# Another search for the order of 18,000 instructions in a one-core attention and MLP kernel

## The chip, the cores and the metric

The kernel runs on one core of a Trainium2 chip. A core has five engines with a queue of instructions each: TensorE (PE in the rows; its weight loads are PEld), VectorE (DVE), ScalarE (ACT), GpSimd (POOL) and SyncE (SP, which here only issues DMAs). The metric is the device time of one execution in microseconds (us), smaller is better. The kernel before takes 666.7 us (median of 3 runs, 666.36 to 667.87).

## The reference

Three layers over a sequence of S = 576 rows, 4 batches, 8 heads of 64 features (512 in all):

```python
def attn(q, k, v):                       # B, H, S, D = 4, 8, 576, 64; scale = 1/8
    q_d, k_d, v_d = (mean over groups of 4 rows)           # 144 rows
    out_up = repeat(softmax(scale * q_d @ k_d.T) @ v_d, 4)
    scores = where(abs(i - j) < 4, scale * q @ k.T, -1e9)
    return out_up + softmax(scores) @ v

def moe(x, w_ch1, w_ch2):                # 512 -> 2048 -> 512
    u = x + real(fft(fft(x, axis=1), axis=2))
    un = (u - mean(u)) / sqrt(var(u) + 1e-6)
    return u + maximum(un @ w_ch1, 0) @ w_ch2

def moe2(x, w_val, conv_w, w_out):       # causal convolution of 5 taps over the rows
    gate = sigmoid(conv(x, conv_w))
    return (gate * (x @ w_val)) @ w_out
```

## The kernel before, in words

Features lie on partitions, rows along the free axis. The MLP and what follows work in twelve units of 192 rows, three for each batch. The first unit's MLP (lines 1160 and 1171) takes float32 operands; the other eleven split every operand into two float16 halves and sum three products (lines 1196 and 1216, products of 192 columns).

The weights come as 64-bit floats. A float32 weight is put together out of the two 32-bit words by three VectorE instructions on 128x1024 integers, here called words: a first step, a TENSOR_SCALAR (`word_op`, line 547), and two SCALAR_TENSOR_TENSOR (helper `stt`, line 448). The tiles are W and X (X_125, X_126 and W_118 to W_123 hold raw weights, W_114 to W_117 the first matrix's float32 words).

Before the first unit can start, batch 0 has to pass attention, transform and mean. This start-up is the function `chain0`, and its steps are:

- local attention in three groups of windows, of 64-row products: scores (line 1439, dS, loads of k in kTa and q in X), maximum (1452), exponentials on ScalarE (1462, dP and its sums dsu), norm on VectorE (1467, 1468 and the helper at 451), turn by TensorE (1476, dPT) and copy (1479), values (1495, dO), and the addition to x on VectorE (454);
- coarse attention for four pairs of heads: sums over four rows (1510, qkT), scores (1518, sc), maximum (1525, nm), exponentials on ScalarE (1534, E, sums lsu), norm, turn (1549, eT), copy by ScalarE (1552, ET), values (1558);
- sums over v and a covariance (1572 to 1585, cv) that scale the float16 halves, folds (1601, fF), halves (FH, FL), the transform over features (1627, ab), mirrored rows (1637 and 1638, mir), the transform over rows (1665), the mean (1707, st), and u (1711).

The coarse norm is the one step of this part that runs on GpSimd (G); V is VectorE:

```python
def coarse_norm(a):
    s_, E = lr["su", a], lr["E", a]
    V.tensor_scalar(out=s_, in0=s_, scalar1=1e-9, scalar2=None, op0=ALU.add)
    V.reciprocal(out=s_, in_=s_)
    for par in range(2):
        mul(G, E[:, par], E[:, par], s_[:, par].unsqueeze(2).to_broadcast([QC, 2, SD]))
```

The order in which every engine works is not left to a scheduler. The program is built as a list of 692 parts, each a step of this kind, and a table ORDER holds for each of the five engines a list of part numbers (`n.a-b` takes the instructions a to b of part n on that engine). Each instruction is chained behind the one ahead of it in that list by a dependency that needs no semaphore. So the table is the order of the five queues, and the waits between engines come on top from the data.

```python
    for name, eng in engines.items():
        line = []
        for x in ORDER[name].split():
            ...
        for x, y in zip(line, line[1:]):
            tc.add_manual_dep(y, x.name, mybir.DependencyInfo(
                mybir.DependencyClass.NoSync, mybir.DependencyReason.DATA), reason="order")
```

Of the kernel before, what the change touches and what calls it, by code (L numbers as in the profile page):

```python
# [80 lines left out]
263.1 296.2 291.2 302 296.1 291.3 394.0 265.0 288.3 265.2 298.3 265.1 288.0 263.3 265.3 306 315 267.0-1 319 269.0-1  # L81
295.0 267.2 269.2 296.0 301 327 272.0 288.1 272.1 274.0 288.4 274.1 288.5 298.2 275.0 288.2 275.1 311 298.0-1 289.3
277.0-1 289.0 277.2 289.1 289.4-5 289.2 277.3 278 394.1 283.0-1 318.0-1 283.2 334 330 283.3-4 286.0 291.4 286.1-2
342.0 314 342.1 318.2 283.5 303.0 305.0 283.6 290.2 290.1 320.1 346 320.3 290.0 318.3 321.1 321.3 303.1 320.0 320.2
323.1 305.1 349 321.0 331 325.0 324 356 321.2 323.3 323.0 323.2 325.1 326.3 326.1-2 326.0 333 394.2 363 339.0 336.0
339.1-2 336.1 325.2-3 347.0 347.3 347.2 337.1 337.0 339.3 348.3 348.2 348.0 351.0 370 394.3 351.2 347.1 339.4 348.1
339.5-7 358 351.3 337.2-3 378 384 353.2-3 339.8-9 368.3 394.4 351.1 368.0 353.0-1 339.10 388 316 368.1 368.4 368.2
368.5 369.0 372.3 396 372.0 364.0 369.1 374.0 393.0 364.1 372.1-2 372.4-5 393.1 400.1 402.1 376.0 374.1 376.3 383.2-3
405 399 376.1 406.1 376.2 376.4-5 380.3 380.0 400.0 400.3 416 413 380.1 402.0 380.2 380.4-5 374.2-3 426 374.4 383.0
406.0 390.0 383.1 387.0-1 418 391.0 429 387.2 390.1 391.2 390.2 391.1 390.3 387.3 391.3 390.4 395.1 395.0 390.5-6  # L90
398.0-1 395.2 390.7 398.2 390.8 522.0 432 390.9 400.2 404 446.1 374.5 435 402.3 402.2 410.1 406.2-3 374.6 390.10 408
439 407 446.0 410.0 410.3 441 410.2 411.0 411.2 411.1 443 522.1 411.3 430.0 414 457 423.0 436.0-1 423.1 428.1 428.0
430.1 449 446.2 436.2-3 422 436.4 428.2 455 428.3 436.5 434.1 444.1 436.6 434.0 444.3 436.7 425 447.1 458 444.0 444.2
462 436.8 447.0 447.3 447.2 450.3 450.2 450.1 522.2 453.3 450.0 453.2 453.1 436.9-11 434.2-3 453.0 451.1 451.0 463.0
460.0 436.12-13 466 468 460.1 522.4 436.14 451.2-3 473 463.1 478 483.0 486.3 486.0 489 480 481.0 486.4 486.1 486.5
481.3 481.2 488.3 427 492.3 492.0 486.2 483.1-2 504 483.3 492.1 499 483.4 488.2 492.4 492.2 492.5 495.0 503 483.5-8
488.0 490.3 497.3 497.0 495.1 509 506.2 483.9 522.3 497.4-5 497.1-2 495.2 490.0 490.2 481.1 502.3 502.0 495.3 488.1
483.10 490.1 514 494.3 494.0 506.3 506.0 502.4 495.4 494.1-2 502.1 502.5 502.2 517 506.1 524 521.0 513.0-2 521.1 507.0
# [1832 lines left out]
```

## Time and profile before

| | |
|---|---|
| median of 3 runs | 666.7 us (666.36 to 667.87) |
| the profiled execution | 668.18 us |
| its span in the profile | 666.4 us |
| mean granted TensorE clock | 0.985 of full speed |
| TensorE busy | 647.4 us (97%), 7751 products |
| VectorE, ScalarE, GpSimd busy | 458.3, 328.5, 127.1 us |
| DMA | 52.08 MB, 79 GB/s over the span |

The span is what the profiler saw between the first and the last instruction; the execution's time has 1.8 us more around it. Every position below is in us from the start of the span. Records of one line that follow each other are put into one row of a timeline with their count, and the brackets at its end say how long the engine had been idle and who released it.

### The profile page before, as it was taken

What the parts mean: (1) busy time and instruction counts of PE and PEld (TensorE: products, weight loads), DVE (VectorE), ACT (ScalarE), POOL (GpSimd) and SP (SyncE); (2) the same over time, 40 slices, a digit from 0 to 9 for tenths busy, and PEclk for the clock granted to TensorE, in tenths of its full rate; (3) what the DMA queues carried; (4) which work ended last, traced back from release to release, by engine and by line L of the source; (5) the groups of instructions that cost most, each with busy time, mean ns of one, the idle gap of its engine ahead of it and who ended that gap; (6) DMA issues with size and microseconds to landing.
All of it is one profiled execution on the core that took longest, in us unless ns stands there. A gap on an engine that the chain in (4) does not pass through costs nothing.

```text
span 666.4 us, 18165 instructions
## 1 busy us (share of the span) xinstructions
PE 647.4 (97%) x7751; PEld 581.6 (87%) x7751; DVE 458.3 (69%) x950; ACT 328.5 (49%) x997; POOL 127.1 (19%) x178
## 2 busy tenths in 40 slices
PE   8968999999999999999999999999999999999997
PEld 4647799999998887989988898998999989999895
DVE  3679999989998877657876645675447763562344
ACT  3665577888334757675235576643232313312122
POOL 0240306321210613501110352030001020000000
PEclk9959999999999999999999999999999999999999
DMA  8976072313424001403240020000300000000001
GB/s 301 402 247 243 2 253 82 101 34 100 161 60 171 20 18 46 142 1 104 77 150 2 27 62 17 3 1 25 116 2 17 2 1 33 1 2 18 2 32 48
DMA packets 23299, 52.08 MB, mean 78 GB/s; under 512 B 1855, under 2 KB 11071, under 8 KB 22194
## 3 DMA queue, kind: packets, MB, share of 16 engines
q1 hardware_dynamic: 23218, 50.91, 22.4%
q8 instruction: 61, 1.00, 0.6%
q14 instruction: 20, 0.16, 0.1%
HBM read 44.41 MB, written 8.26 MB: 79 GB/s over the span
## 4 chain that ended last, share of the span: by engine, by line
PE 78%; DVE 11%; issue 5%; DMA 3%; POOL 2%; ACT 1%; SPq 0%; POOLq 0%; ACTq 0%
PE ph L1196 25%; PE pc L1216 24%; PE out L1324 7%; PE val L1308 7%; DVE W L448 5%; PE ab L996 2%; POOL E L451 1%; PE dO L805 1%; PE po L1572 1%; PE st L1080 1%; PE sc L883 1%; DMA raw<-in_moe_w_ch_dram 1%; PE pc L1171 1%; DMA kTa<-in_k_dram 1%; PE dPT L788 1%
## 5 line engine op out<-in xcount | busy, mean ns | idle before, releaser
L1196 PE MATMUL ph<-uh,W 128*128 128x192 f16 x1408 | 198.3, 246 | 1.3 <-DVE hl L448 0.7
L1196 PEld LDWEIGHTS <-W 128*128 128x128 f16 x2112 | 176.8, 98 | 9.5 <-issue 4.3
L1216 PE MATMUL pc<-hh,W 128*128 128x192 f16 x1232 | 171.7, 246 | 0.0
L1196 PE MATMUL ph<-ul,W 128*128 128x192 f16 x704 | 171.2, 246 | 0.0
L1216 PEld LDWEIGHTS <-W 128*128 128x128 f16 x1848 | 154.3, 98 | 5.7 <-issue 1.4
L1216 PE MATMUL pc<-hl,W 128*128 128x192 f16 x616 | 129.5, 246 | 0.0
L1200 ACT ACTIVATE hh<-ph 128x384 f16<-128x384 f32 x88 | 42.7, 488 | 125.8 <-PE ph L1196 100.5
L448 DVE SCALAR_TENSOR_TENSOR hl<-ph,hh 128x384 f16<-128x384 f32 x88 | 48.2, 552 | 77.6 <-ACT hh L1200 77.4
L448 DVE SCALAR_TENSOR_TENSOR W<-X,cw,W 128x192 f32<-128x192 f32 x160 | 64.1, 437 | 2.7 <-ACT W L1271 2.3
L1308 PE MATMUL val<-yy,W 128*128 128x192 f16 x576 | 59.6, 246 | 0.5 <-ACT yy L1250 0.5
L1308 PEld LDWEIGHTS <-W 128*128 128x128 f16 x576 | 48.5, 98 | 1.1 <-issue 0.4
L1324 PE MATMUL out<-W,gh 128*128 128x512 f16 x144 | 46.5, 379 | 0.0
L769 ACT ACTIVATE dP<-dS,dmx 128x64 f32<-128x64 f32 x120 | 36.2, 329 | 0.6 <-PE dPT L788 0.3
L448 DVE SCALAR_TENSOR_TENSOR W<-W,W 128x1024 int32<-128x1024 int32 x24 | 29.5, 1237 | 0.1
L451 POOL TENSOR_TENSOR E<-E,lsu 72x288 f32<-72x288 f32 x16 | 18.9, 1197 | 55.1 <-ACT nm L1529 19.7
L454 POOL TENSOR_TENSOR sq<-sq 128x384 f32<-128x384 f32 (+1 forms) x12 | 10.6, 880 | 93.6 <-ACT sq L1091 93.2
L1324 PE MATMUL out<-W,gl 128*128 128x512 f16 x72 | 27.1, 379 | 0.0
L769 ACT ACTIVATION_READ_ACCUMULATOR dP<-dS,dmx 128x1 f32 x120 | 26.7, 223 | 0.0
L1324 PEld LDWEIGHTS <-gh 128*128 128x128 f16 x144 | 14.0, 98 | 12.0 <-issue 0.2
L1216 PE MATMUL pc<-hh,Wz 128*128 128x192 f16 x176 | 24.3, 246 | 0.0
L1171 PE MATMUL pc<-h,W 128*128 128x192 f32 x128 | 23.3, 329 | 0.0
L1160 PE MATMUL ph<-u,W 128*128 128x192 f32 x128 | 22.5, 327 | 0.4 <-DVE u L1711 0.4
(288 smaller groups left out, 1212.0 us busy)
## 6 DMA issues: line engine op xcount, KB each, us to landing
W<-in_moe_w_ch_dram SPq DMA_DIRECT2D x12, 1024.0 KB
out_dram<-osb SPq DMA_DIRECT2D x17, 256.0 KB
vw<-in_vw_dram SPq DMA_DIRECT2D x8, 512.0 KB
v<-in_vp_dram SPq DMA_DIRECT2D x24, 144.0 KB
X<-in_q_dram SPq DMA_DIRECT2D x6, 576.0 KB
kT<-in_k_dram SPq DMA_DIRECT2D x4, 582.0 KB
X<-in_moe_w_ch_dram SPq DMA_DIRECT2D x2, 1024.0 KB
raw<-in_moe_w_ch_dram SPq DMA_DIRECT2D x4, 512.0 KB
```

Of the source, the lines that this page charges most:

```text
L448: return eng.scalar_tensor_tensor(out=out, in0=in0, scalar=scalar, in1=in1, op0=op0, op1=op1)
L451: return eng.tensor_tensor(out=out, in0=a, in1=b, op=ALU.mult)
L454: return eng.tensor_tensor(out=out, in0=a, in1=b, op=ALU.add)
L769: A.activation(out=s_[:, z, a], in_=pss[par][:, z, a], func=AF.Exp, scale=SCALE, bias=mx[:, par, z, a:a + 1], accum_out=su[:, par, z, a:a ...
L996: T.matmul(out=ps[0:n, c0:c1], lhsT=d[x][:, c, sd, e, n0:n0 + n], rhs=feat[:, w, c, c0:c1], start=(t == 0), stop=(t == 5),)
L1160: T.matmul(out=ps[:, e], lhsT=W[AT[kc * 2 + m // 8] + 1][:, o:o + 128], rhs=u()[:, kc, :], start=(kc == 0), stop=(kc == 3))
L1171: T.matmul(out=c["ps"][m // 2][:, m % 2], lhsT=W[9 + g][:, o:o + 128], rhs=hs[g // 2][:, g % 2, e, :], start=(kk == 0 and m % 2 == 0), sto ...
L1196: T.matmul(out=ps[:, e], lhsT=w1_ap(pw, kc, 2 * g + e), rhs=uh[px][:, kc, :], start=(t == 0), stop=(t == 11))
L1200: A.activation(out=h_, in_=ps, func=AF.Relu)
L1216: T.matmul(out=ps[m // 2][:, m % 2], lhsT=w2_ap(pw, kk, m), rhs=x[px][:, e, :], start=(kk == 0 and (pw, px) == (0, 0) and m % 2 == 0), sto ...
L1308: T.matmul(out=ps[:, e], lhsT=wv_ap(pw, kc, 2 * mh + e), rhs=m_["y"][px][:, kc, :], start=(t == 0), stop=(t == 11))
L1324: T.matmul(out=ps, lhsT=(gh, gl)[px][:, kc, t * 128:(t + 1) * 128], rhs=wo_ap(pw, kc), start=(n == 0), stop=(n == 11))
```

## The change

Only the table ORDER changes: all five lists are other orders of the same parts. No instruction's shape, engine or operands change, and no tile is placed elsewhere. Because the table became 14 lines longer, each line number after it is larger by 14 in the changed kernel. One line of the diff stands for the rest:

```diff
     "vector": """
-21 20 30 18 25 32.0-1 32.3 32.2 41 48.0 38.1 38.0 48.1 28 23 27 58.0 54 65 58.1 0 31 71 77.1 77.0 60 34 81.0 85.0 81.1
...
```

On SP, the second load of k is now asked for ahead of the first of q, the table for the transform over features goes from behind six weight loads to ahead of all of them, and the weight loads change places. GpSimd's coarse norms stay in their order. On TensorE the turns and values of the second and third local groups follow each other as before, and the first mirrored products come ahead of the transform over features, the others in the middle of it.

The first place is VectorE's queue around the last of the four coarse norms (its sums are lsu_552, its reciprocal releases GpSimd), up to the norm of the second local group (dsu_342). W and X are words; f2_v0, f2s_v0, p2a and p2b are one-element-wide steps that find a scale, tot is in PSUM. Before:

```order
L515 TENSOR_REDUCE f2_v0_559<-tot_557 128x1
L1539 TENSOR_SCALAR lsu_552<-lsu_552 72x4
L517 TENSOR_SCALAR f2s_v0_561<-f2_v0_559 128x1
L1540 RECIPROCAL lsu_552<-lsu_552 72x4
L547 TENSOR_SCALAR W1_114<-X_126 128x1024
L547 TENSOR_SCALAR W3_115<-W19_123 128x1024
L448 SCALAR_TENSOR_TENSOR W1_114<-X_126,W1_114 128x1024
L448 SCALAR_TENSOR_TENSOR W3_115<-W19_123,W3_115 128x1024
L547 TENSOR_SCALAR W5_116<-W11_119 128x1024
L448 SCALAR_TENSOR_TENSOR W1_114<-X_126,W1_114 128x1024
L448 SCALAR_TENSOR_TENSOR W5_116<-W11_119,W5_116 128x1024
L1467 TENSOR_SCALAR dsu_342<-dsu_342 128x16
```

And now:

```order
L1553 TENSOR_SCALAR lsu_552<-lsu_552 72x4
L462 SCALAR_TENSOR_TENSOR cw_108<-craw_109,cw_108 128x20
L1554 RECIPROCAL lsu_552<-lsu_552 72x4
L561 TENSOR_SCALAR W5_116<-W9_118 128x1024
L529 TENSOR_REDUCE f2_v0_559<-tot_557 128x1
L531 TENSOR_SCALAR f2s_v0_561<-f2_v0_559 128x1
L462 SCALAR_TENSOR_TENSOR W3_115<-W19_123,W3_115 128x1024
L513 TENSOR_SCALAR p2a_565<-f2s_v0_561 128x1
L462 SCALAR_TENSOR_TENSOR W5_116<-W9_118,W5_116 128x1024
L561 TENSOR_SCALAR W7_117<-W15_121 128x1024
L515 TENSOR_SCALAR p2b_567<-p2a_565 128x1
L1481 TENSOR_SCALAR dsu_342<-dsu_342 128x16
```

Seven word operations stood between the reciprocal and the local group's norm, without anything between them; now there are four, and the scale's small steps stand between them.

The second place is VectorE's queue a little earlier, around the covariance's first reader (tr from cv) and the norms of the second and third coarse pairs (lsu_379, lsu_499). Before:

```order
L547 TENSOR_SCALAR W1_114<-X_125 128x1024
L451 TENSOR_TENSOR tr_459<-cv_414,eye_102 128x128
L1539 TENSOR_SCALAR lsu_379<-lsu_379 72x4
L1540 RECIPROCAL lsu_379<-lsu_379 72x4
L1525 TENSOR_REDUCE nm_478<-sc_472 72x2
L1525 TENSOR_REDUCE nm_478<-sc_473 72x2
L606 TENSOR_REDUCE ss_v0_461<-tr_459 128x1
L470 MEMSET ones_105 128x128
L448 SCALAR_TENSOR_TENSOR W1_114<-X_125,W1_114 128x1024
L1539 TENSOR_SCALAR lsu_499<-lsu_499 72x4
L1540 RECIPROCAL lsu_499<-lsu_499 72x4
```

And now:

```order
L561 TENSOR_SCALAR W1_114<-X_125 128x1024
L462 SCALAR_TENSOR_TENSOR W1_114<-X_125,W1_114 128x1024
L462 SCALAR_TENSOR_TENSOR W3_115<-W17_122,W3_115 128x1024
L1553 TENSOR_SCALAR lsu_379<-lsu_379 72x4
L462 SCALAR_TENSOR_TENSOR cw_108<-craw_109,cw_108 128x20
L561 TENSOR_SCALAR W7_117<-W13_120 128x1024
L465 TENSOR_TENSOR tr_459<-cv_414,eye_102 128x128
L1554 RECIPROCAL lsu_379<-lsu_379 72x4
L484 MEMSET ones_105 128x128
L1539 TENSOR_REDUCE nm_478<-sc_472 72x2
L1539 TENSOR_REDUCE nm_478<-sc_473 72x2
L561 TENSOR_SCALAR W1_114<-X_126 128x1024
```

Words have come ahead of tr. From the start up to the last pair's lsu_552 there are ten word operations (five first steps, five others) where there were four (two and two); reductions still follow the reciprocals of the second and third pair.

The third place is ScalarE's queue around the copies of the last pair's turned E (ET_606, ET_613) and the exponentials of the second local group (dP_344, dP_353). Before:

```order
L1462 ACTIVATE dP_344,dsu_342<-dS_246,dmx_291 128x64 x4
L1462 ACTIVATE dP_353,dsu_342<-dS_248,dmx_291 128x64
L1560 ACTIVATE base_136<-po_594 128x144
L1462 ACTIVATE dP_405,dsu_394<-dS_308,dmx_384 128x64
L1552 ACTIVATE ET_606<-eT_601 72x288
L1462 ACTIVATE dP_353,dsu_342<-dS_248,dmx_291 128x64
L1552 ACTIVATE ET_613<-eT_608 72x288
L1462 ACTIVATE dP_344,dsu_342<-dS_246,dmx_291 128x64 x3
L1462 ACTIVATE dP_353,dsu_342<-dS_248,dmx_291 128x64 x3
L1560 ACTIVATE base_136<-po_615 128x144
```

And now:

```order
L1476 ACTIVATE dP_344,dsu_342<-dS_246,dmx_291 128x64
L1476 ACTIVATE dP_353,dsu_342<-dS_248,dmx_291 128x64 x2
L1574 ACTIVATE base_136<-po_594 128x144
L1566 ACTIVATE ET_606<-eT_601 72x288
L1476 ACTIVATE dP_344,dsu_342<-dS_246,dmx_291 128x64 x2
L1566 ACTIVATE ET_613<-eT_608 72x288
L1476 ACTIVATE dP_344,dsu_342<-dS_246,dmx_291 128x64 x2
L1476 ACTIVATE dP_396,dsu_394<-dS_306,dmx_384 128x64
```

Of the second group's sixteen exponentials four now stand behind the first copy, where seven stood.

## Rows read from the trace of the kernel before

**Rows 1.** The page: busy time of each engine, and TensorE in the 40 slices.
```profile
PE 647.4 (97%) x7751; PEld 581.6 (87%) x7751; DVE 458.3 (69%) x950; ACT 328.5 (49%) x997; POOL 127.1 (19%) x178
...
PE   8968999999999999999999999999999999999997
```

**Rows 2.** The chain that ended last: start us, us, what.
```profile
93.18 7.09 DMA raw<-in_moe_w_ch_dram
...
639.37 5.94 PE pc L1216 x72
```

**Rows 3.** TensorE's waits from 79 us on: us in total, times, longest.
```profile
PE ph L1196 <- DVE hl L448: 0.7, 1, 0.7
...
PE dPT L788 <- DVE dP L451: 0.3, 1, 0.3
```

**Rows 4.** Windows: stretch, us, busy by engine, granted clock, DMA share, GB/s.
```profile
32.00:52.00 20.00, 14.17 (x150) 10.78 (x150) 15.38 (x33) 12.58 (x67) 9.18 (x3) 0.50 0.70 230
54.00:60.00 6.00, 4.16 (x39) 3.11 (x36) 5.92 (x14) 3.04 (x7) 0.00 (x0) 1.00 0.76 271
60.00:70.00 10.00, 9.68 (x115) 8.29 (x113) 10.00 (x15) 6.71 (x15) 0.03 (x1) 1.00 0.66 242
70.00:79.00 9.00, 8.43 (x86) 6.16 (x84) 8.19 (x19) 4.74 (x12) 5.09 (x13) 1.00 0.01 3
130.00:662.00 532.00, 529.91 (x6526) 485.07 (x6525) 351.02 (x776) 246.42 (x707) 91.54 (x134) 1.00 0.14 46
...
45.00:75.00 30.00, 27.14 (x340) 22.16 (x337) 29.70 (x57) 20.28 (x52) 3.08 (x8) 0.88 0.40 145
79.00:127.00 48.00, 47.85 (x458) 46.24 (x458) 46.15 (x59) 33.56 (x101) 14.38 (x16) 1.00 0.38 134
```

**Rows 5.** GpSimd's timeline, 26 to 43 us.
```profile
27.37 1.29 POOL L451 TENSOR_TENSOR E<-E,lsu 72x288 f32<-72x288 f32 x2 [4.96 <-ACT ET L1552]
30.94 2.94 POOL L451 TENSOR_TENSOR E<-E,lsu 72x288 f32<-72x288 f32 x2 [2.28 <-DVE lsu L1540]
34.42 7.30 POOL L451 TENSOR_TENSOR E<-E,lsu 72x288 f32<-72x288 f32 x2 [0.54 <-DVE lsu L1540]
```

**Rows 6.** VectorE's timeline, 26 to 78 us.
```profile
26.65 0.29 DVE L451 TENSOR_TENSOR tr<-cv,eye 128x128 f32<-128x128 f32 x1 [2.58 <-PE cv L1585]
...
27.67 0.82 DVE L1525 TENSOR_REDUCE nm<-sc 72x2 f32<-72x288 f32 x2 [0.44 <-PE sc L1518]
...
33.79 0.16 DVE L515 TENSOR_REDUCE f_v<-tot 128x1 f32<-128x1 f32 x1 [0.44 <-PE tot L509]
...
34.07 0.17 DVE L1540 RECIPROCAL lsu<-lsu 72x4 f32<-72x4 f32 x1
34.17 0.66 DVE L547 TENSOR_SCALAR W<-X 128x1024 int32<-128x1024 int32 x1
...
39.36 1.21 DVE L448 SCALAR_TENSOR_TENSOR W<-W,W 128x1024 int32<-128x1024 int32 x1
44.76 0.18 DVE L1467 TENSOR_SCALAR dsu<-dsu 128x16 f32<-128x16 f32 x1 [4.19 <-ACT dP L1462]
...
77.99 0.95 DVE L1711 TENSOR_TENSOR u<-X,st 128x768 f32<-128x768 f32 x1 [0.40 <-PE st L1707]
```

**Rows 7.** TensorE's timeline, 41 to 80 us.
```profile
41.15 1.32 PE L1549 MATMUL eT<-eye,E 72*72 72x72 f32 x8 [4.50 <-POOL E L451]
...
46.56 2.06 PE L1476 MATMUL dPT<-eye,dP 128*128 128x128 f32 x8 [0.41 <-DVE dP L451]
48.54 2.29 PE L1495 MATMUL dO<-PT,vw 64*64 64x58 f32 x64
...
52.63 2.00 PE L1495 MATMUL dO<-PT,vw 64*64 64x58 f32 x64
...
79.00 1.24 PE L1160 MATMUL ph<-u,W 128*128 128x192 f32 x6 [0.41 <-DVE u L1711]
```

**Rows 8.** ScalarE's timeline, at the copy of the turned E.
```profile
41.88 0.41 ACT L1552 ACTIVATE ET<-eT 72x288 f32<-72x288 f32 x1 [4.58 <-PE eT L1549]
```

More of the change, by code (lines that the diff above doesn't have):

```diff
@@ new lines @@
+229.1 229.0 183.3 217.0-2 229.2 230.1 217.3 211.2 231.0 230.0 230.2 231.1 241.1 241.0 249.1 249.0 259.1 255 121 259.0
+267 286.0 269 272 274.1 274.0 275 277 286.1-2 283.0 286.3 283.1-3 278.1 283.4 290.0 283.5-6 290.1 283.7-8 290.2 278.0
+339.0-1 318.1 318.0 290.3 286.4 339.2-3 325.1 325.0 359.1 359.0 359.2 337.1 337.0 360.1 360.0 361 362.1 360.2 362.0
+362.2 390 395 398 407 408 404 411 428.1 428.0 414 434 483.0 472.0-1 475.1 451 472.2 475.0 475.2 483.1 476 483.2-3 307
+477.1 477.0 477.2 530.0-1 519 530.2-3 523 534.1 537.0 534.0 529 417 537.1 538 543 593 623
@@ L82 @@
[L82 to L86, printed above, removed]
@@ new lines @@
+120.0 120.6 120.1-3 120.17 120.7-8 120.4 120.9 120.5 120.10-11 127.0-6 127.12 127.7-9 127.13-15 127.24 127.10-11
+127.16-23 127.25-35 126.1-3 141.0-7 142.9 142.0 142.10-11 142.1 142.12-13 142.2-8 142.14-17 141.8 148.0-14 183
+148.15-17 151 192.1 158 192.3 192.5 192.0 192.2 192.7 192.9 161 162 192.4 192.6 192.8 192.10 192.12 192.14 192.11
+192.13 192.15 192.17 192.16 193.0 184 193.1-3 191 166.0-2 194.0-2 196.0-2 218.0 218.2 166.3 196.3-7 194.3-6 218.3
+194.7 197.1 197.0 197.2-27 197.29 197.28 197.30-31 197.33 197.32 207.0-1 200.0-2 218.6 218.1 218.4 193.4-7 200.3-6
@@ new lines @@
+207.2-7 213.0-2 218.5 218.7 200.7 223.2 215 210.0-3 213.3 223.3 223.0-1 223.4-6 210.4-7 223.7 227.0-1 227.4-5 227.2-3
+232.0-1 232.4-5 234.0-1 234.4-5 227.6-7 216.1 216.0 216.2-9 216.11 216.10 216.12-24 213.6 213.4-5 213.8-9 213.7
+213.10-19 216.26 216.25 216.27 216.29 216.28 216.31 216.33 216.30 216.32 232.2-3 250.0-16 237.0 251.0-10 232.6
+251.11-20 237.1 237.4-5 232.7 234.2-3 234.6 242.0 234.7 250.17-23 251.21-23 236.4-5 236.0-1 236.6 237.2-3 237.6-7
+257.0-10 242.2-3 242.1 242.6 217 236.7 236.2-3 242.4-5 242.7 231.1 231.0 231.2-3 244.0-1 244.4 244.2 244.5 244.3
@@ new lines @@
+244.6-7 257.11-23 236.8-9 236.12 236.10-11 236.14-15 236.18 236.13 236.16-17 236.19 236.22-23 236.20-21 236.24-36
+236.38-39 236.37 241.1 241.0 241.3 241.2 261.0-14 266.0-6 240.0 266.7-11 256.0 256.6 256.1-2 256.7-9 256.3-5 256.10
+256.12-14 256.11 256.15 256.18 256.16 256.19-21 256.17 256.22-23 266.12-18 260.6 260.0 260.7 260.1-3 260.8 260.4
+260.9-11 260.18 260.5 260.19-20 260.12-14 260.21 260.15-16 261.15-17 260.22 240.1 240.4-5 240.2 240.6-7 261.18-23
+260.17 260.23 266.19-21 240.3 245.0 266.22-23 249.1 249.0 249.3 249.2 240.8-11 264.6 264.0 264.7-9 270.0-12 276.0-2
@@ new lines @@
+246.0-1 276.3-6 245.1 264.1 264.10 276.7-15 246.4 246.2-3 246.5-7 270.13-18 264.11 264.2-4 264.18-19 264.5 264.12
+264.20 264.13 264.21-22 264.14 264.23 264.15-17 246.8 246.10-11 246.14 246.9 246.12-13 246.15 246.18-19 246.16-17
+246.20-36 246.38 246.37 246.39 268.0-3 268.6 268.4 268.7-10 268.5 268.12-13 268.11 268.14-15 268.18 268.16 268.19-22
+268.17 268.23 253 270.19-21 273.6 273.0 273.7 273.1-3 248.0 276.16 270.22-23 273.8-9 273.4 273.10 273.5 273.11-12
+273.18-20 273.13 273.21-22 273.14-15 273.23 273.16-17 276.17-22 279.6 248.4-6 248.1-3 248.7 255.1 255.3 255.0 255.2
@@ new lines @@
+300.9 300.15 300.10-11 300.16 300.18 300.17 300.19-21 319.4-5 272.0 300.22-23 304.0-2 304.6 304.3 304.7-9 304.4-5
+272.1 304.10-11 304.18-19 304.12 304.20-21 304.13 304.22 304.14 272.2-4 304.15-17 304.23 319.6-15 313.6-7 313.0
+319.16-23 313.1 313.8 313.2 313.9 313.3 313.10-11 327.0-12 272.5-6 274.0-3 313.4 313.18 313.5 313.12-14 313.19-20
+313.15 313.21-23 313.16-17 327.13-23 272.7-23 274.4-16 334.0-8 330.0-6 274.17-23 334.9-10 275 322.6 322.0-1 322.7-8
+322.2-4 322.9-11 322.5 322.12-13 322.18-19 322.14 322.20-21 322.15-17 322.22-23 329.6 329.0-2 277.9-11 277.0-7
@@ new lines @@
+464.0 464.6 460.23 466.15 464.7-8 464.1-2 468.4-6 463.22 466.16 463.23 464.3-5 464.9 464.12 464.10 464.13 464.11
+464.18-19 464.14-15 464.20 465.0-2 465.4-7 465.3 468.7-15 464.21 464.16-17 468.16 466.17-21 468.17-22 466.22-23
+464.22-23 468.23 465.8-9 465.12 465.10 465.13 465.16 465.11 465.14 465.17 465.20-21 465.15 465.18-19 465.22-26 465.28
+465.27 465.29-36 465.38-39 465.37 467.6-8 467.0 467.9 467.1-3 467.10 467.4-5 467.11 467.18 467.12 467.19-20 467.13
+467.21 467.14-16 467.22 467.17 467.23 470.0 470.6-8 470.1-5 470.9-13 480.0 470.14 470.18 470.15-16 470.19-20 470.17
@@ new lines @@
+470.21-23 480.1-2 471.6 471.0-1 471.7-9 471.2-3 471.10-11 471.4-5 471.12 471.18-20 471.13-14 471.21 471.15-17
+471.22-23 478.0-9 469.4 478.10-23 469.0-1 469.5-6 469.2 469.7 469.3 480.3-23 469.8-9 469.12-13 469.10-11 469.14-29
+469.32 469.30-31 469.33-34 469.36 469.35 469.37-39 486.0-1 486.3 486.2 499.0-2 483.0 489.0-15 499.3-7 487.0-9
+489.16-23 485.0 485.6 485.1 485.7 485.2-3 487.10-11 485.8-9 485.4-5 485.12-14 485.10-11 485.15-16 485.18-19 485.17
+499.8-12 485.20-22 504.0-2 483.1 485.23 493.0 493.6 493.1-2 492 504.3-11 499.13-18 493.7-8 493.3-4 493.9 493.5 493.12
@@ new lines @@
+511.12-14 511.20 511.15 511.21 511.16 511.22 502.0-1 502.3 502.2 511.17 524.0 517.17-20 500.0 500.4 500.1 500.5
+500.2-3 500.6-7 511.23 517.21-23 515.6 515.0-4 515.7-10 515.5 515.11 515.18 515.12 515.19 500.8-11 524.1 515.20-21
+515.13-14 515.22 515.15 515.23 515.16-17 518.0 518.6 518.1-3 518.7-11 518.18 518.4-5 518.12 518.19-20 518.13 518.21-22
+518.14-16 518.23 518.17 520.0-1 524.2-19 526.0-1 505.0-1 505.4 505.2 505.5-7 505.3 524.20-21 526.2-11 505.8-11 520.2-6
+520.12 520.7-11 520.13-14 520.18-23 520.15 507.0-5 526.12-21 524.22-23 520.16-17 510.0-5 507.6 510.6 507.7-23
@@ new lines @@
+551.9 548.10-13 560.1 555.14-15 554.19 554.12 554.20 554.13-15 554.21 537.13 555.16-22 551.10-12 554.22 554.16
+537.14-15 554.17 554.23 551.13 560.2-4 537.16-20 555.23 537.21-22 548.14 538.0 551.14-16 556.6-7 556.0-2 556.8-9 556.3
+556.10 556.4-5 556.11-12 556.18 556.13 556.19-20 538.1 537.23 562.0-5 538.2-4 556.14 556.21 556.15-16 556.22 556.17
+556.23 551.17 548.15-16 557.0 551.18 557.6 557.1-3 560.5 557.4-5 557.12-13 557.7-8 557.14 557.9 557.15 557.10 557.16
+557.11 557.18-19 557.17 557.20 551.19 538.5 560.6-12 557.21-23 560.13-23 562.6-20 538.9 538.6 538.10 551.20-22
@@ new lines @@
+603.18-19 603.17 603.20-23 608.6-7 608.0 608.8 608.1-2 608.9 608.3 608.10 608.4 608.11 608.18 608.5 608.12-15
+608.19-21 609.0-14 595.7-8 612.0-8 608.22 608.16-17 609.15 612.9-12 609.16 608.23 611.6 611.0 611.7 611.1 611.8
+611.2-3 609.17-18 595.9-11 612.13-15 609.19-21 611.9-11 611.18 611.4-5 611.12-14 611.19 611.15-16 606.6 609.22-23
+611.20-21 606.7-11 612.16-20 614.0-3 612.21-23 614.4-23 611.22-23 611.17 613.6-7 613.0 613.8 613.1 613.9-10 613.2-4
+613.11 610.0 607.0-11 621.0-1 613.5 610.1-3 619.0-1 613.12 613.18 613.13 613.19-20 610.4-7 613.21-22 613.14 621.2-3
@@ L296 @@
+665.18-19 664.9-11 665.20 665.17 665.21-23 667.6 668.11-23 670.0-5 667.7 667.0 667.8-9 667.1 667.10-11 667.18 667.2-5
+667.12 667.19-20 667.13-16 667.21-23 667.17 670.6-20 674.0-4 670.21-23 669.0-1 669.6 669.2 669.7-10 669.3-5 669.12-13
+669.11 669.14-15 669.18-21 669.16 669.22 669.17 669.23 671.6-8 671.0-1 671.9-10 671.2-5 671.11-12 671.18-22 671.13-17
+671.23 672.0 674.5-6 672.12 672.1-11 672.13-23 674.7-11 675.0-5 674.12-21 675.6-9 689.0 675.10-23 685 689.1-23
+674.22-23 688 687 690 691
 """,
```

406 lines of the change are left out of this document (182 added, 224 removed), and 8 rows, old and new, of the table ORDER.

## The prediction

> **What bounds the kernel now.** I began with the page. TensorE is busy for 647.4 of the 666.4 us of the span, and in the forty slices only the first few and the last are below 9 tenths [rows 1]. The reader is to see that there's no slack to win anywhere but in the first four or five slices. Second, the chain that ended last: in its late part it's one TensorE run after another (72 products of one weight block in 5.94 us, 82.5 ns each), so the end is the start of the dense part plus a fixed amount of product work [rows 2]. Third, TensorE's waits behind 79 us: six in 583 us, the longest 0.7, together 2.7 us [rows 3]. So with W = 79.00, when the first product of the MLP starts [rows 7], the end is W plus a stretch in which TensorE hardly stops: 529.9 of 532 us from 130 on [rows 4]. A microsecond off W is a microsecond off the kernel, as long as the stretch behind it stays without new waits. Everything this change can win lies ahead of 79 us.
>
> Fourth, what sets W. The longest piece of the chain ahead of 79 us, as far as it names an engine, is GpSimd's pair of multiplications of the last coarse softmax (E, line 451). So I went to the timelines. The last three of these pairs, all of the same shape, take 1.29, 2.94 and 7.30 us [rows 5]. What differs is VectorE: behind the reciprocal at 34.07 seven word operations (32-bit shifts and ands that build float32 weights) run back to back from 34.17 to 40.57, and GpSimd's first multiplication is through only half a microsecond behind their end [rows 5, 6]. TensorE stands for 4.50 us for that E [rows 7], ScalarE's copy of the turned E for 4.58 [rows 8], and since the exponentials of the second local group stand behind that copy on ScalarE, VectorE itself then has nothing for 4.19 us [rows 6]. VectorE's stall is the dear one: from 45 to 75 us it's 29.70 of 30 us busy [rows 4], so whatever it loses before, it loses for good.
>
> **The change, part by part.** Nothing is computed anew; the five engines' queues get another order. VectorE and the two engines that wait for it decide.
>
> *Words ahead of the last coarse norm.* Before, two first steps and two second or third steps of words are done ahead of it (the order shows it); now five and five. The seven in the row cost 6.4 us: three of about 0.6 and four of about 1.14 from start to start. So 3 x 0.6 + 3 x 1.14 = 5.2 us are moved forward. VectorE has 2.58 us of wait for the covariance there, and three of 0.44 to 0.50 [rows 6], 3.96 us in all, that this work fills. The rest, 1.2 us, delays the last reciprocal: 34.07 + 1.2 = 35.3. If the first waits of the start-up shrink because the second k load is now asked for earlier on SP's queue, it's up to 0.6 less. I take 35.1. The covariance's own reader, and the second head pair's norm behind it, then stand behind word steps that fit the 2.58 us almost to the tenth: from no delay to 0.9 us, already within the 1.2.
>
> *The last coarse norm.* Before, seven word operations stand behind the reciprocal; now one of 0.66, then a reduce that reads PSUM and a one-element operation, and only then the next long one. I expect GpSimd to get in there: first multiplication through at 35.1 + 0.1 + 0.66 + 0.5 = 36.4, the second at 37.0, against 41.72: 4.7 us earlier. If the next word operation gets in between the two, it's 1.2 us later, 38.2, which is 3.5 earlier. VectorE pays for it by waiting for one or both multiplications, 0.65 to 1.3 us; before it paid nothing for this pair. The other two pairs now have PSUM reductions of 0.82 us behind their reciprocals, as the pair of 1.29 us has [rows 5, 6], and the pair that took 2.94 should take about 1.3.
>
> The Trainium skill (SBUF — State Buffer, section "SBUF: two separate sides") says that VectorE and GpSimd share one port pair as an exclusive lock that an instruction holds to its end, and that the other engine is blocked until then. The trace agrees that it's blocked, not slowed; it does not agree that the lock is open again at each instruction's end, as the first multiplication sat through seven of them. By the page's wording it would have been done near 35.5 already, and this hole wouldn't exist; that is the last rival below.
>
> *The second local group.* Its exponentials now stand for the most part ahead of the copies of the turned E on ScalarE; four are behind the first copy, where seven stood. With E at 37.0, the turn (1.32 us) and these, they're done near 39.5. VectorE gets to that group's sums at 35.9 + 1.0 (GpSimd) + two long words, one short and small change (3.0) = 39.9, against 44.76. Its 4.19 us stall is gone, with two short and one long word operation (2.3 us) more behind it. The turn of that group (dPT) goes from 46.56 to 41.7, and the last values, which end at 54.63, to near 49.7 [rows 7]: 4.9 us.
>
> *From there to W.* Two floors. VectorE: 44.76 to 77.99 less its 0.4 at the end [rows 6] is 32.8 us; less 2.3, and less 0.6 for a word operation that is now behind u, 29.9; from 39.9 this gives u at 69.8 plus some 0.8 of waits, 70.6, 7.4 earlier. TensorE: from 54.63 to 79.00 is 24.4 us, of which 22.3 are busy [rows 4]; from 49.7 it gives W between 72.0 and 74.1, 4.9 to 7.0 earlier. TensorE's floor is the later one, so it counts. I take 5.5, in its lower half, since the folds and the mirrored products still wait for VectorE's additions, and the GpSimd fight may cost a microsecond.
>
> *Behind W.* Product work is the same. The order of the six waits changes; the two in the rows lie behind VectorE [rows 3]. Bounds: all 2.7 us gone, or the same again. I take nothing.
>
> *SP, and the rest of GpSimd's queue.* The table for the transform over features goes ahead of the weights, and the weights are loaded in about the order in which they're now built. If one lands late, VectorE waits at a first step of words; the bound is the time of one such step at either side, 0.6 us. I take nothing.
>
> Sum: 5.5 us. The profiled execution took 668.18 us (666.4 of span and 1.8 around it), 1.5 over the median; 668.18 - 5.5 = 662.7, and from the median 666.7 - 5.5 = **661.2**. Its own range is 659.7 to 662.7 (4.0 to 7.0).
>
> **The rivals.**
> 1. *GpSimd does not get in.* The opening behind the one word operation is two tiny operations, 0.2 us. If VectorE holds on through them, the pair waits for three more words (1.14 + 1.14 + 0.6) and is done near 39.5: 2.2 us earlier than before, and VectorE's stall shrinks by about as much. For: VectorE held on seven times in a row. Against: the pair went through at once beside reductions that read PSUM [rows 5, 6]. 666.7 - 2.2 = 664.5. Chance 0.15.
> 2. *The gain is eaten behind W.* From 79 to 127 us VectorE is busy for 46.15 of 48 us [rows 4], a transfer of 7.09 us stands in the chain [rows 2], and TensorE already waits for a VectorE product there [rows 3]. If W comes 5.5 us earlier but the words of the second weight matrix only half as much, 2.7 us come back as waits at the local scores or the first float16 unit. 661.2 + 2.7 = 663.9. Chance 0.12.
> 3. *More.* The clock is at half (granted 0.50) from 32 to 52 us [rows 4]. If, with no 4.5 us hole, it comes back earlier, TensorE's floor falls below VectorE's: 7.4 earlier, and with the 0.6 of the earlier load 8.0: 658.7. Chance 0.08.
> 4. *Slower: the clock comes back later.* It rose where the values of the two last groups had run nearly without a break from 48.54 on, and stayed at 1.00 though TensorE was then busy for only 4.16 of 6 us [rows 4, 7]. If the new order breaks that run up, since VectorE feeds it piece by piece, the mirrored products and the transform behind it run at half. Each microsecond of the 22.3 us of work there costs one more; from 5.5 us on it turns the gain into a loss. At a third of it (7.4 us): 661.2 + 7.4 = 668.6. Against it: the two runs of values and the turn between them stand in the same order on TensorE as before. Chance 0.08.
> 5. *The hole is not VectorE's.* If something else held GpSimd's operation, it stays where it is, and the time is 666.7. For: by the lock as the page has it, seven instructions can't hold it. Against: in both slow pairs it ended half a microsecond behind the last word operation. Chance 0.07.
>
> **How the numbers follow.** The forecast has 0.50. Faster by over 0.2% (1.3 us, about what a measurement of this kernel can tell from no change): forecast and rivals 1 to 3, 0.85. Within: rival 5, 0.07. Slower: rival 4, 0.08. The range reaches from 658.0, under rival 3, to 666.0, over rival 1; rivals 4 and 5 and a little at either end are left out, under 0.2.
>
> **What would show it.** Right: the last pair on GpSimd takes under 3.5 us and ends by 38.5; TensorE's wait for E is below 1 us; VectorE's wait for the second group's exponentials is gone; u near 72, W near 73.5; the rest of the span 587 us as before. Rival 1 shows a pair of over 4 us; 2 shows W as forecast and new waits between 73 and 130 us; 3 and 4 show in the granted clock from 30 to 70 us; 5 shows the pair long with VectorE idle. The prediction is wrong if W moves by less than 4 us, or if the span behind W grows by over 1.5.

## The result, and the profile after

The changed kernel takes **670.95 us** (median of 5 runs, 669.79 to 672.18) against 666.7 before: a ratio of 1.006, 95% interval 1.0041 to 1.0078. It's slower by 4.2 us where 5.5 us less were forecast. (In two later series of runs the kernel before took 667.32 and 667.22 us, so differences across series are good to about half a microsecond; each ratio below is to the kernel before of its own series.) The profiled execution took 672.18 us, with a span of 670.4.

One part went the way forecast, though by less: the first product of the MLP starts at 77.01 us, 2.0 us earlier than in [rows 7]. Then it's all lost again. From there to the end of the span there are 593.4 us, where there were 587.4. TensorE's timeline of the changed kernel:

```profile
32.63 0.70 PE L1563 MATMUL eT<-eye,E 72*72 72x72 f32 x4 [3.23 <-POOL E L465]
...
77.01 2.28 PE L1174 MATMUL ph<-u,W 128*128 128x192 f32 x13
```

TensorE's waits from 75 us on in the changed kernel (us in total, times, longest):

```profile
PE ph L1210 <- DVE hl L462: 2.1, 2, 1.2
PE ab L1010 <- ACT FH L993: 1.3, 1, 1.3
PE val L1322 <- DVE yy L462: 1.1, 1, 1.1
PE dS L769 <- DMA X<-in_q_dram: 1.1, 1, 1.1
PE st L1089 <- DVE u L1725: 0.5, 1, 0.5
PE st L1094 <- DVE uc L468: 0.5, 1, 0.5
PE ph L1210 <- DVE ul L1139: 0.4, 1, 0.4
PE val L1322 <- DVE W L462: 0.3, 1, 0.3
```

They add up to 7.3 us; before there were 2.7 [rows 3]. No single one is large. Of these kinds three were there before, for hl (0.7), yy (0.5) and u (0.4); the others are new. Windows show where they lie. First the changed kernel (stretch, us, busy by engine, clock, DMA share, GB/s):

```profile
150.00:200.00 50.00, 47.80 (x648) 45.91 (x647) 45.34 (x105) 25.70 (x63) 10.72 (x14) 1.00 0.33 107
200.00:250.00 50.00, 47.66 (x597) 41.74 (x596) 40.61 (x74) 23.80 (x64) 16.68 (x29) 1.00 0.22 77
...
340.00:420.00 80.00, 77.69 (x1085) 68.42 (x1083) 51.28 (x110) 47.38 (x171) 24.02 (x29) 1.00 0.17 59
```

The same stretches of the kernel before:

```profile
150.00:200.00 50.00, 49.32 (x666) 47.46 (x664) 48.98 (x111) 26.72 (x66) 10.47 (x14) 1.00 0.33 107
200.00:250.00 50.00, 48.59 (x615) 43.14 (x613) 41.85 (x76) 29.58 (x86) 15.81 (x31) 1.00 0.20 69
...
340.00:420.00 80.00, 80.00 (x1123) 71.30 (x1120) 48.45 (x116) 46.45 (x172) 22.36 (x29) 1.00 0.09 28
```

TensorE (the first busy time) stands for 6.9 us in these three stretches, and stood for 2.1. The reader should also look at the third number, VectorE: in the first two stretches it's less busy than before, 45.3 against 49.0 and 40.6 against 41.9 of 50 us. So there it isn't short of time; it waits.

Now the start-up, where 5.5 us were to come from. GpSimd's timeline of the changed kernel, against [rows 5]:

```profile
21.05 1.74 POOL L465 TENSOR_TENSOR E<-E,lsu 72x288 f32<-72x288 f32 x2 [19.61 <-DVE lsu L1554]
27.86 4.72 POOL L465 TENSOR_TENSOR E<-E,lsu 72x288 f32<-72x288 f32 x2 [5.08 <-DVE ones L484]
35.85 1.29 POOL L465 TENSOR_TENSOR E<-E,lsu 72x288 f32<-72x288 f32 x2 [3.27 <-ACT base L1574]
39.94 2.54 POOL L465 TENSOR_TENSOR E<-E,lsu 72x288 f32<-72x288 f32 x2 [2.80 <-DVE lsu L1554]
```

The last pair takes 2.54 us where it took 7.30, as forecast. But it comes so late that it ends at 42.48, behind the 41.72 of before, because the hole has moved: the second pair, 1.29 us before, takes 4.72. VectorE's timeline of the changed kernel says why:

```profile
28.37 0.82 DVE L1539 TENSOR_REDUCE nm<-sc 72x2 f32<-72x288 f32 x2 [0.52 <-PE sc L1532]
29.11 0.68 DVE L561 TENSOR_SCALAR W<-X 128x1024 int32<-128x1024 int32 x1
29.71 2.35 DVE L462 SCALAR_TENSOR_TENSOR W<-X,W 128x1024 int32<-128x1024 int32 x2
35.30 0.17 DVE L1553 TENSOR_SCALAR lsu<-lsu 72x4 f32<-72x4 f32 x1 [3.25 <-ACT E L1548]
```

A row of three word operations starts at 29.11. The pair's second multiplication, in a row of its own when the window is narrow, had started at 28.48:

```profile
28.48 4.10 POOL L465 TENSOR_TENSOR E<-E,lsu 72x288 f32<-72x288 f32 x1
```

Unhindered it takes 0.66 us and would have been done at 29.15. It was done at 32.58, 0.52 us behind the row's end at 32.06. TensorE then waits 3.23 us for that E, ScalarE's copy of it 3.58, the exponentials behind the copy are late, and VectorE itself stands for 3.25 us at the third norm. It is the old chain of [rows 5 to 8], one pair earlier.

### The profile page after: what moved, and what is told of

It is laid out like the page before. It is cut to its first block, busy times and chain, and to the rows that moved or that the text cites. A ratio compares the mean times of both kernels' runs of the same rounds, so it can differ in the third digit from the quotient of the medians.

```text
span 670.4 us, 18154 instructions
## 1 busy us (share of the span) xinstructions
PE 651.0 (97%) x7751; PEld 581.7 (87%) x7751; DVE 457.2 (68%) x950; ACT 327.7 (49%) x997; POOL 126.2 (19%) x178
## 3 DMA queue, kind: packets, MB, share of 16 engines
q1 hardware_dynamic: 23218, 50.91, 22.3%
## 4 chain that ended last, share of the span: by engine, by line
PE 82%; DVE 9%; DMA 3%; POOL 2%; ACT 1%; issue 1%; SPq 1%; DVEq 0%; POOLq 0%; ACTq 0%
PE ph L1210 24%; PE pc L1230 23%; PE out L1338 7%; PE val L1322 6%; PE pc L1185 3%; PE ph L1174 2%; DVE W L462 2%; PE ab L1010 2%; DMA X<-in_q_dram 2%; PE po L1586 1%; PE dO L819 1%; PE po L1432 1%; PE sc L897 1%; PE st L1094 1%; PE po L942 1%
## 5 line engine op out<-in xcount | busy, mean ns | idle before, releaser
L1210 PE MATMUL ph<-uh,W 128*128 128x192 f16 x1408 | 204.0, 246 | 2.1 <-DVE hl L462 2.1
L1230 PE MATMUL pc<-hh,W 128*128 128x192 f16 x1232 | 175.2, 246 | 0.0
L1322 PE MATMUL val<-yy,W 128*128 128x192 f16 x576 | 63.5, 246 | 1.4 <-DVE yy L462 1.1
L1285 ACT ACTIVATE W<-X,cw 128x192 f32<-128x192 f32 x40 | 16.8, 450 | 12.8 <-DVE gl L462 6.3
```

The costliest lines, as they stand in the source:

```text
L1210: T.matmul(out=ps[:, e], lhsT=w1_ap(pw, kc, 2 * g + e), rhs=uh[px][:, kc, :], start=(t == 0), stop=(t == 11))
L1230: T.matmul(out=ps[m // 2][:, m % 2], lhsT=w2_ap(pw, kk, m), rhs=x[px][:, e, :], start=(kk == 0 and (pw, px) == (0, 0) and m % 2 == 0), sto ...
L1285: A.activation(out=m, in_=x, func=AF.Copy, scale=w)
L1322: T.matmul(out=ps[:, e], lhsT=wv_ap(pw, kc, 2 * mh + e), rhs=m_["y"][px][:, kc, :], start=(t == 0), stop=(t == 11))
```

## The experiments

Orders can be spliced: all instructions that one execution had started by some instant form a set that waits for nothing outside it, so one order can be followed for that set and another for the rest.

**The new start-up alone, and the new rest alone.** Each list of ORDER is cut where u is formed. In words, not as a diff of the table:

```text
first run:   new order up to u, then the order of before, less what is already in it
second run:  order of before up to u, then the new order, less what is already in it
```

> The changed order up to u on all five engines, the order of before for everything behind it. Theory A (the new order behind u costs some 6 us, the new start-up wins 2.0): 664.7 us, first MLP product near 77.0 us, waits behind it about 3 us as in the kernel before. Theory B (the stretch behind u cannot use an earlier start, whichever order it has): 666 to 667, with some 2 us more of waits behind u than before. Theory C (both): 665.5.

Measured: 664.68 us (664.45 to 664.95) against 667.32, ratio 0.9963 (0.9951 to 0.9975). TensorE's first product of the MLP, and its waits behind u in this run:

```profile
75.51 2.87 PE L1161 MATMUL ph<-u,W 128*128 128x192 f32 x16 [0.47 <-DVE u L1712]
```
```profile
PE ph L1197 <- DVE hl L449: 0.7, 1, 0.7
PE ph L1197 <- ACT uh L1125: 0.6, 1, 0.6
PE val L1309 <- ACT yy L1251: 0.5, 1, 0.5
PE pq L1020 <- ACT DS L1047: 0.2, 1, 0.2
```

The first product comes 1.5 us earlier than the changed kernel's 77.01, with the same order up to u. But 1.1 us of that are there at the first coarse pair already (GpSimd starts it at 19.97 here and at 21.05 there), so a position in one profile compares with that in another to about a microsecond, unless their first pairs start together.

> The order of before up to u, the changed order behind it. Theory A: the first MLP product near 79.0, waits behind it of 7 to 9 us, time 672.5 to 673. Theory B (the waits come only because u is earlier): waits behind u of about 7 us or less, and the time equals the changed kernel's 670.95 or is below it, down to 667.

Measured: 672.55 us (672.33 to 674.14) against 667.32, ratio 1.0086 (1.0072 to 1.01). TensorE's first product of the MLP, and its longest waits behind u:

```profile
79.34 0.98 PE L1172 MATMUL ph<-u,W 128*128 128x192 f32 x5
```
```profile
PE ph L1208 <- DVE hl L460: 2.1, 2, 1.2
PE dS L767 <- DMA X<-in_q_dram: 1.1, 1, 1.1
PE val L1320 <- DVE yy L460: 1.1, 1, 1.1
```

So the change is two changes of opposite sign: a start-up that wins 2.6 us and a rest that costs 5.2. Theory B falls: with the old order an earlier u is a whole gain (the waits of the first run are those of before), and with the new order most of the waits stand there though u is as late as before, 5.4 us in all. That is less than the 7 to 9 that theory A gave, because two of them do hang on an earlier u: the one for FH shrinks from 1.3 to 0.1 us and the one for uc from 0.5 to under 0.1. So the two parts don't simply add: -2.6 and +5.2 make 2.6, and the changed kernel is slower by 4.2 us (3.6 against the kernel before of these runs). With the new rest the new start-up is worth only about 1.6 us (672.55 to 670.95).

**The new order up to 150 us.** The same splice with the cut at 150 us.

> The changed order for all that it had started by 150 us, the order of before behind that. The changed kernel waited for only 0.3 us between 77 and 150 us, and for 8.3 us behind. Theory A with the cost behind 150 us: as the first run, 664.7, plus or minus 0.7. If the order between 77 and 150 us carries the debt (it puts off work that is missed later): 667 or more.

Measured: 665.0 us (664.17 to 665.44), ratio 0.9967 (0.9955 to 0.9979), and the same four waits as in the first run. The loss is in the order behind 150 us, which agrees with the windows above. (They show 6.9 us of TensorE's idle time behind 150 us; no view shows the 8.3 of the expectation.)

**Four repairs behind u.** The changed kernel; each piece moves an instruction out from behind one that waits:

```diff
 (VectorE)
-SCALAR_TENSOR_TENSOR W13_120<-W15_121,s_w2_1465,W13_120 128x1024
 TENSOR_TENSOR ul_1735<-uc_1710,uh_1734 128x768
 SCALAR_TENSOR_TENSOR hl_2503<-ph_2476,hh_2501 128x384
 SCALAR_TENSOR_TENSOR hl_2380<-ph_2353,hh_2378 128x384
+SCALAR_TENSOR_TENSOR W13_120<-W15_121,s_w2_1465,W13_120 128x1024
...
+SCALAR_TENSOR_TENSOR hl_6485<-ph_6458,hh_6483 128x384
 TENSOR_SCALAR r0_6193<-vv_6191 128x192
 TENSOR_TENSOR r1_6194<-r0_6193 128x192
 SCALAR_TENSOR_TENSOR r1_6194<-r1_6194,vv_6191 128x192
-SCALAR_TENSOR_TENSOR hl_6485<-ph_6458,hh_6483 128x384
 (ScalarE)
+ACTIVATE FH_2097<-fF_2168,s_x1_1904 128x2x289
 ACTIVATE yy_2794<-X_132,s_y0_2680 128x768
 ACTIVATE hh_3049<-ph_3024 128x384
-ACTIVATE FH_2097<-fF_2168,s_x1_1904 128x2x289
 (SP)
+DMA X_4898<-in_q_dram 128x2x576
 DMA dx_4366<-X_2937 1x576
...
 DMA kT_4931<-in_k_dram 128x1164
+DMA X_4898<-in_q_dram 128x2x576
...
-DMA X_4898<-in_q_dram 128x2x576
...
-DMA X_4898<-in_q_dram 128x2x576
```

What stood behind these four is read in the changed kernel's timelines. VectorE, at 161 us:

```profile
161.75 1.79 DVE L462 SCALAR_TENSOR_TENSOR bq<-f2s_v,ff 128x1 f32<-128x1 f32 x1
...
163.83 1.27 DVE L462 SCALAR_TENSOR_TENSOR W<-W,s_w,W 128x1024 f16<-128x1024 f32 x1
...
165.89 1.01 DVE L462 SCALAR_TENSOR_TENSOR hl<-ph,hh 128x384 f16<-128x384 f32 x2
```

and GpSimd beside it:

```profile
160.60 1.75 POOL L465 TENSOR_TENSOR E<-E,lsu 72x288 f32<-72x288 f32 x2 [6.72 <-ACT ET L937]
162.31 1.21 POOL L468 TENSOR_TENSOR X<-X,base 128x576 f32<-128x576 f32 x1
```

A one-column step, 0.14 to 0.15 us at its three other places, takes 1.79 us and ends with GpSimd's addition (163.54 and 163.52); the two hl, whose inputs were ready at 164.7 and 165.5, come behind that and a weight split, and TensorE stands for 0.87. By these ends it's GpSimd that holds VectorE here, the reverse of the start-up. For the loads of q, the chain that ended last in the changed kernel has

```profile
338.46 10.79 DMA X<-in_q_dram
```

SP had stood until 334.23 us at a load of k, at the end for 8.2 us with TensorE as the releaser; nine transfers were then asked for within 4.2 us and shared the DMA engines. The q in question was the last of the nine.

> The changed kernel with four repairs behind u, each of one or two instructions moved a few rows up on one engine: VectorE's two hl ahead of a 1.3 us weight split (165 us) and one hl ahead of a step of the variance that GpSimd held for 1.5 us (411 us), ScalarE's FH ahead of yy that waits for VectorE (188 us), SP's two loads of q ahead of a load that waits for its buffer (310 and 334 us). Theory A (the debt is these waits, each an instruction that stands behind one that waits): the four waits of 0.87, 1.33, 1.08 and 1.24 us fall to under 0.4 each, time 670.95 - 4 = 667 (666 to 668). Rival S (TensorE is then held by the next late instruction, the stretch has no slack): waits reappear within 10 us of each, time 669 to 671.

Measured: 667.31 us (666.44 to 668.45) against 667.22 before, ratio 1.0 (0.9991 to 1.0008): 3.6 us less than the changed kernel's 670.95. TensorE's waits behind u:

```profile
PE val L1322 <- DVE yy L462: 1.1, 1, 1.1
PE pc L1230 <- DVE hl L462: 0.9, 1, 0.9
PE eT L932 <- POOL E L465: 0.5, 1, 0.5
PE ph L1210 <- DVE ul L1139: 0.4, 1, 0.4
PE val L1322 <- DVE W L462: 0.4, 1, 0.4
```

All four waits, 4.5 us together, are gone. Theory A holds, with a part of S: two new waits of 0.9 and 0.5 us are there. Of those that weren't touched three are as they were, and the one for uc is gone too. The debt isn't paid in full: this kernel has the new start-up, and with the old rest that start-up takes 664.68 us (first run), so the repaired rest still costs some 2.6. The four were tried together, so what each is worth by itself isn't shown.

**One reduction in the start-up.** The first run's kernel (new start-up, old rest) with

```diff
 TENSOR_REDUCE nm_478<-sc_472 72x2
 TENSOR_REDUCE nm_478<-sc_473 72x2
+TENSOR_REDUCE ss_v0_461<-tr_459 128x1
 TENSOR_SCALAR W1_114<-X_126 128x1024
...
-TENSOR_REDUCE ss_v0_461<-tr_459 128x1
```

> As the first, and one VectorE reduction of 0.27 us (ss_v from tr) moved from behind the third coarse maximum to behind the second, so that it stands between the second coarse norm and three word operations. Theory L (GpSimd's second multiplication was caught 0.04 us before its end, because the first word operation started then, and it then sits through the whole row): its pair falls from 4.72 to about 1.3 us, TensorE's wait of 3.2 us for it goes, the first MLP product comes 2 to 3 us earlier than in the first run, time 662 to 663. Rival R (the pair was held by something else, or VectorE is the floor anyway): pair still over 4 us or no earlier u, time as the first run's.

Measured: 663.35 us (661.29 to 664.46), ratio 0.9937 (0.9921 to 0.9953). GpSimd's timeline:

```profile
26.98 1.29 POOL L452 TENSOR_TENSOR E<-E,lsu 72x288 f32<-72x288 f32 x2 [5.07 <-DVE ones L471]
31.83 3.42 POOL L452 TENSOR_TENSOR E<-E,lsu 72x288 f32<-72x288 f32 x2 [3.56 <-DVE lsu L1541]
37.45 2.54 POOL L452 TENSOR_TENSOR E<-E,lsu 72x288 f32<-72x288 f32 x2 [2.20 <-DVE lsu L1541]
```

0.27 us of other work in front of the words frees the second pair: 4.72 to 1.29. The third pair is now caught instead (3.42), since its reduction stood there before. The first product comes at 74.08, against 75.51 in the first run: 1.4 us of the expected 2 to 3, because VectorE still stands at the last norm, for 2.8 us. The cause is on ScalarE: the last of the four exponentials that it waits for stands behind the copy of the caught pair's E.

**And one exponential.** To the kernel just shown (the expectation calls it the third run's), on ScalarE, in addition:

```diff
 ACTIVATE E0_551,lsu_552<-sc_535,nm_540 72x144
+ACTIVATE E0_551,lsu_552<-sc_535,nm_540 72x144
 ACTIVATE ET_578<-eT_573 72x288
-ACTIVATE E0_551,lsu_552<-sc_535,nm_540 72x144
```

> The third run's kernel (new start-up with the reduction moved, old order behind u), and on ScalarE the last of the four exponentials of the last coarse pair moved ahead of the copy of the third pair's turned E (ET_578), behind which it stood for 2.16 us. Theory L: VectorE's 2.2 to 2.8 us of idle time ahead of the last norm goes, the last GpSimd pair ends some 2 us earlier, first MLP product 1.5 to 2.5 us earlier than in the third run, time 661 to 662. Rival: GpSimd's third and fourth pair now collide with the words back to back and give the 2 us back: 663 to 664.

Measured: **662.21 us** (661.2 to 662.92) against 667.22, ratio 0.9923 (0.9909 to 0.9936), the lowest of all versions: 5.0 us less than before and 8.7 less than the changed kernel. GpSimd's last pairs, and TensorE's first product:

```profile
31.85 2.95 POOL L452 TENSOR_TENSOR E<-E,lsu 72x288 f32<-72x288 f32 x2 [3.56 <-DVE lsu L1541]
35.21 1.56 POOL L452 TENSOR_TENSOR E<-E,lsu 72x288 f32<-72x288 f32 x2 [0.41 <-DVE lsu L1541]
```
```profile
72.68 2.87 PE L1161 MATMUL ph<-u,W 128*128 128x192 f32 x16 [0.46 <-DVE u L1712]
```

The first product comes 1.4 us earlier than with the reduction alone, where 1.5 to 2.5 were expected, and here the first pairs start together (20.19 and 20.18). The times of the two kernels overlap (661.2 to 662.92 and 661.29 to 664.46), so what this move is worth stands on the profile. The third pair is still caught, for 2.95 us.

**The hold by itself.** The kernel before with two one-column steps moved into the row of seven words:

```diff
 RECIPROCAL lsu_552<-lsu_552 72x4
 TENSOR_SCALAR W1_114<-X_126 128x1024
+TENSOR_SCALAR p2a_565<-f2s_v0_561 128x1
 TENSOR_SCALAR W3_115<-W19_123 128x1024
+TENSOR_SCALAR p2b_567<-p2a_565 128x1
 SCALAR_TENSOR_TENSOR W1_114<-X_126,W1_114 128x1024
...
-TENSOR_SCALAR p2a_565<-f2s_v0_561 128x1
...
-TENSOR_SCALAR p2b_567<-p2a_565 128x1
```

> The kernel before with two one-column VectorE steps (p2a and p2b, 0.14 us each) moved up into the row of seven word operations, behind its first and its second. Theory L (an operation of GpSimd that is held gets in only where VectorE's row of two-port operations is broken by one that doesn't hold the port, however short): GpSimd's pair falls from 7.30 to 2 to 3 us, TensorE's wait of 4.50 us to under 1, VectorE's stall of 4.19 to under 1, first MLP product 3 to 4 us earlier, time 663 to 664. Rival R (the pair is held by the sum of the work, not by the row's unbrokenness): pair over 6.5 us, time 666.5 to 667.

Measured: 663.91 us (663.07 to 664.04) against 667.22, ratio 0.9945 (0.9933 to 0.9958). GpSimd's last pair, and VectorE's row:

```profile
33.66 2.00 POOL L451 TENSOR_TENSOR E<-E,lsu 72x288 f32<-72x288 f32 x2 [2.69 <-DVE lsu L1540]
```
```profile
33.41 0.66 DVE L547 TENSOR_SCALAR W<-X 128x1024 int32<-128x1024 int32 x1
33.99 0.14 DVE L499 TENSOR_SCALAR p2a<-f2s_v 128x1 f32<-128x1 f32 x1
34.06 1.09 DVE L547 TENSOR_SCALAR W<-W 128x1024 int32<-128x1024 int32 x1
35.07 0.14 DVE L501 TENSOR_SCALAR p2b<-p2a 128x1 int32<-128x1 int32 x1
35.13 1.62 DVE L448 SCALAR_TENSOR_TENSOR W<-X,W 128x1024 int32<-128x1024 int32 x1
```

The pair goes from 7.30 to 2.00 us, TensorE's wait for it and VectorE's stall of 4.19 are gone (TensorE waits 1.7 us for the local group's norm instead), and the first product comes at 74.84, 4.2 us earlier, of which 1.3 are there at the first pair already (19.86 against 21.12). GpSimd gets in at each of the two tiny steps, and the word operation behind each is 0.41 us longer (1.09 for the 0.68 of an undisturbed first step, 1.62 for 1.21). Two rows moved on one engine are worth 3.3 us, no less than the whole new start-up with its 2.6.

## Why the prediction was wrong, step by step

Both signs that were named for being wrong came: W moved by 2.0 us, under 4, and the span behind it grew by 6.0, over 1.5.

*What bounds the kernel* was right: time is the start of the MLP plus the stretch behind it. With the old order behind u, the profiled executions end 588.5 to 589.1 us behind the first product (72.68, 74.08, 74.84 and 75.51 go with 661.2, 663.1, 664.0 and 664.5), against 589.2 before. The condition that was set with it, no new waits behind u, is what broke.

*Words ahead of the last norm.* Forecast: reciprocal at 35.1. Measured: 39.59. The words did fit into the covariance's wait, but the reciprocal came behind the caught second pair.

*The last coarse norm* was right in how long it takes, by its second case: a word operation gets in between the two multiplications, and the pair takes 2.54 us, under the 3.5 that were named as the sign of it. TensorE's wait for its second half is 0.91 us. Its place was wrong: it ends at 42.48, not by 38.5. Rival 1 falls with that. Rival 5 falls too: the run with one reduction moved and the run with two tiny steps show the hold to be VectorE's row. By the Trainium skill (SBUF — State Buffer, "SBUF: two separate sides") the lock is held for the whole instruction. Here the multiplication was held through seven of them, for 6.68 us, and came through where the row was broken, so the measurement decides.

*The second local group.* Forecast: its norm at 39.9. Measured: 44.35, against 44.76 before. Its own stall is gone, but the 3.25 us at the third norm took its place. *From there to W* was about right: from this norm to u 31.2 us, where 30.7 were forecast and 33.2 were before. So u comes 2.4 us earlier, 0.4 won ahead of this norm and 2.0 behind it. (The 22.3 us in TensorE's floor count from 54 us; from 54.63 on it's 21.6.)

*The other two pairs* is the first step that failed. "The pair of 1.29 us has a reduction of 0.82 behind it, so these take 1.3" took the presence of a reduction for enough. For this pair it's how long the other work lasts that counts: from the reciprocal's end to the end of the second multiplication took 1.43 us where nothing hindered it, and the words began 1.40 us behind the reciprocal. Before, a reduction of 0.27 us more stood there; my text did not price it. The change moved the hole instead of closing it: 2.6 us (first run) for 5.5. With one reduction and one exponential moved, the start-up wins 5.0, near the forecast, so the sum's other terms were together of about the right size.

*Behind W: "I take nothing"*, within 2.7 us either way, is the second step that failed, and the one that turned the sign: 5.2 us by the second run, and 6.0 in the changed kernel's profile. The bounds came from the waits that were there, which say nothing of a new order's waits. Rival 2 named the direction, but as a lack of VectorE time between 73 and 130 us; the waits lie between 150 and 420 us, from 150 to 250 us VectorE has more idle time than before, and most of them don't need an earlier u. Each of the four that were repaired was one or two instructions in line behind another that waits or is held. I had read the new order by rows for the start-up alone.

*The clock* (rivals 3 and 4): it didn't come back later, so rival 4 falls. In the changed kernel it was granted at half from 31 to 48 us, where it was from 32 to 52 before [rows 4], and in full behind that (1.00 from 48 to 60):

```profile
31.00:48.00 17.00, 13.21 (x98) 9.22 (x99) 12.43 (x31) 12.57 (x71) 5.41 (x5) 0.50 1.04 338
```

That is the direction of rival 3, but not its gain. Whether the 4 us at full clock are a part of the 2.0 was not separated; VectorE was busy for 29.5 of the 30 us from 45 to 75.

What stays open: the new order's stretch behind u is 6.0 us longer, but its waits only 4.6. The other 1.4 us are TensorE's own busy time, for the same 7003 products. Windows of the kernel before and of the changed one:

```profile
79.00:666.00 587.00, 581.32 (x7003) 534.31 (x7003) 400.66 (x839) 283.46 (x821) 108.23 (x151) 1.00 0.17 55
77.00:670.00 593.00, 582.72 (x7003) 534.12 (x7001) 397.70 (x838) 282.87 (x821) 111.49 (x151) 1.00 0.16 54
```

It's there in the second run (582.5) and in the repaired kernel (582.2) as well, so it goes with the new order behind u; why the same products take longer in it wasn't tried. Nor was why some waits came back in other places after the repairs.

## What to carry to other kernels

When an order is changed everywhere, cut it in two by a splice and time the halves before explaining the sum: here +5.2 and -2.6 looked like one small loss, and what was left over between their sum and the whole showed that one part hangs on the other. A GpSimd operation that VectorE's long steps hold up wants a gap in VectorE's row as long as itself or a tiny step between the long ones, and what it holds up is found by following the instructions that stand behind its reader on each engine. In a stretch where one engine has no slack, look in every queue for an instruction that others need and that stands in line behind one that waits; moving it a few rows gave back 3.6 us here for 4.5 us of waits.

## What the runs showed that I hadn't expected

- A multiplication on GpSimd that had been on its way for 0.63 of its 0.66 us was still held for the whole row of words. In the single records the held ones end 0.52 to 0.53 us behind the last word operation, however long they had run before: 32.06 to 32.58 in the changed kernel, 34.11 to 34.63 in the run with one reduction moved.
- Being done before the words begin isn't the whole rule. In the run with two tiny steps the third pair took 1.29 us, with the same neighbours as the pair of 2.94 before [rows 5]: a word operation began when the second multiplication had run for 0.43 us, and it was the word that waited (0.78 us instead of 0.68). In the run with one reduction moved a multiplication that had run for 0.46 us was held, for 2.80. So tens of nanoseconds may decide over microseconds, and which engine waits in such a case is not explained by these runs.
- A VectorE step of one column, 0.14 us long, lets GpSimd in; the end of a GpSimd multiplication and the addition of 1.21 us behind it in turn held such a step for 1.65 us.
